# Ordering every engine queue of a chunked-attention and MLP kernel with a list scheduler inside the kernel, and loading v as fp32 with a cast on GpSimd

## The chip, the cores and the metric

The kernel runs on one core of a Trainium2 chip. The time is the device time of one execution in microseconds (us). "Before" has a median of 350.23 us in three executions (348.98 to 351.46). Ratios below are the mean time of one kernel's fast runs over the mean time of the other's fast runs of the same rounds, with a 95% interval, so they are not quite the ratios of the medians that are quoted beside them.

Engines are named as in the profile: PE is the matrix engine (TensorE), PEld its weight loads, DVE is VectorE, ACT is ScalarE, POOL is GpSimd, SP is SyncE, which here only starts transfers. "Granted clock" is the share of full speed that the throttle of PE allowed. The trace records it from some time after the start only (from 12.4 us in "before"), and the views count the time before that as full clock, although the matmuls there take the durations of half clock. A matmul's end is modelled by the profiler, so distances below are taken from start to start.

The profiled execution of "before" took 353.15 us and is marked slow, about 3 us above the median. So about 3 us of any difference between the two traces may be that.

## The reference

```python
# q, k, v: [4, 8, 768, 64] fp32;  w_in: [512, 2048];  w_out: [2048, 512]
k_min, k_max = min and max of k over each chunk of 32 keys         # 24 chunks
ub  = sum_d max(q * k_min, q * k_max)          # bound of each query for each chunk
ub  = where(chunk of the query >= chunk, ub, -1e9)
sel = the 6 chunks with the largest ub
p   = softmax(q k^T / 8, over selected chunks and keys <= query)
x   = (p v), as [3072, 512]
h   = x @ w_in;   g = h * clip(h + 3, 0, 6) / 6
return g @ w_out
```

Heads are worked on in pairs: there are 16 pairs, four for each batch. For a pair there are these steps, named by a letter in the code: K and Q (transpose the loaded tile, make the chunk minimum and maximum, and the positive and negative parts of q), U (bound matmuls), V (transpose the bounds back, then the top six on DVE), L (transpose the selection and copy it beside q), S (scores, three tiles a head, then exp on ACT and the causal mask on GpSimd) and P (probabilities times v). The MLP of a batch can start when all four pairs of that batch are done. It fills PE while the attention of the next batch goes on.

## The kernel before

Only PE has an order of its own. It is written by hand: lists of attention steps, between which a quota of MLP items is drawn. The order of the other engines is left to the framework. MLP items come only from the second batch on.

```python
ctx.enter_context(tc.manual_schedule(engines={mybir.EngineType.PE}))
...
ORDER = [("S", 0, 0, 0), ("L", 1), ("S", 0, 0, 1), ("P", -1, 1), ("M",), ("U", 2), ...]
FIRST = [("K", 0), ("Q", 0), ("U", 0), ("K", 1), ("V", 0), ("Q", 1), ("L", 0)]
START = [("S", 0, 0, 0), ("U", 1), ("S", 0, 0, 1), ("K", 2), ("V", 1), ...]
...
def run_slot(steps, quota):
    total = sum(c for c, _ in steps)
    done = acc = 0.0
    for c, f in steps:
        f()
        done += c
        while mlp and acc < quota * done / total:   # MLP work, paced by the quota
            cm, fm = mlp.pop(0)
            fm()
            acc += cm
```

The three places where the change also alters the data path:

```python
def load_v(i):                      # v: two transfers a pair, cast to bf16 on the way, GpSimd's queue
    ...
    for e in range(2):
        nc.gpsimd.dma_start(VB[:, e, :, 0:D], v[b, 2 * hp + e].rearrange("(blk p) d -> p blk d", p=P))

    # end of step_Q: the q rows of the score operand, copied on DVE
    for e in range(2):
        nc.vector.tensor_copy(s["RHS"][e][0:D, :], QTS[e * D:(e + 1) * D, 0:S])

def step_L(i):                      # three transposes of 128 columns, four copies
    s = st[i]
    SLT = ps_sm.tile([P, QH], BF16, name="SLT", tag="ps")
    for t in range(NT):
        n = min(P, QH - t * P)
        nc.tensor.transpose(SLT[:, t * P:t * P + n],
                            s["SEL"][0:n, t].rearrange("p h e c -> p (h e c)"), IDENTB[0:n, 0:n])
    with tc.high_priority(offset=HI):
        for h in range(2):
            for e in range(2):
                r = (2 * h + e) * CH
                nc.vector.tensor_copy(s["RHS"][e][D:D + NCH, P + h * QH:P + (h + 1) * QH], SLT[r:r + NCH, :])
```

The softmax here doesn't subtract the row's maximum and nothing guards it: scores larger than these inputs give would overflow.

Of the kernel before, what the change touches and what calls it, by code (L numbers as in the profile page):

```python
# [15 lines left out]
P = 128  # L16
CH = 32
TOPK = 6
BIG = 50.0
E_VAL = 8.0 * BIG  # L20


@with_exitstack
def kernel(
# [21 lines left out]
    NSB = NBLK - 1  # L46
    assert D == 64 and S == 768 and H % 2 == 0 and TOPK * CH >= P
    scale = 1.0 / np.sqrt(D)

    const = ctx.enter_context(tc.tile_pool(name="const", bufs=1))  # L50
    ps_big = ctx.enter_context(tc.tile_pool(name="ps_big", bufs=3, space=bass.MemoryType.PSUM))
    ps_sm = ctx.enter_context(tc.tile_pool(name="ps_sm", bufs=2, space=bass.MemoryType.PSUM))
    src = ctx.enter_context(tc.tile_pool(name="src", bufs=4))
    xpool = ctx.enter_context(tc.tile_pool(name="xpool", bufs=2))
    work = ctx.enter_context(tc.tile_pool(name="work", bufs=2))
    ptpool = ctx.enter_context(tc.tile_pool(name="ptp", bufs=9))
    small = ctx.enter_context(tc.tile_pool(name="small", bufs=4))
    gt_pool = ctx.enter_context(tc.tile_pool(name="gtp", bufs=2))
    u_pool = ctx.enter_context(tc.tile_pool(name="up", bufs=3))
    o_pool = ctx.enter_context(tc.tile_pool(name="op", bufs=3))  # L60

    ctx.enter_context(tc.manual_schedule(engines={mybir.EngineType.PE}))
# [3 lines left out]
    loads = {}  # L66

    def load_qk(i):
        b, hp = pairs[i]
        KS = src.tile([P, NBLK, 2, D], FP32, name="KS", tag="ks")  # L70
        QS = src.tile([P, NBLK, 2, D], FP32, name="QS", tag="qs")
        for t, x in ((KS, k), (QS, q)):
            for e in range(2):
                nc.sync.dma_start(t[:, :, e, :], x[b, 2 * hp + e].rearrange("(blk p) d -> p blk d", p=P))
        loads[i] = [KS, QS, None]

    def load_v(i):
        b, hp = pairs[i]
        VB = VB_tiles[i % NVB]
        for e in range(2):  # L80
            nc.gpsimd.dma_start(VB[:, e, :, 0:D], v[b, 2 * hp + e].rearrange("(blk p) d -> p blk d", p=P))
        loads[i][2] = VB

    IDENT32 = const.tile([P, P], FP32, name="IDENT32")
    load_qk(0)
    make_identity(nc, IDENT32[:])
    QH = NSB * P // 2
    NT = -(-QH // P)
    EMASK = const.tile([P, 2, 2, NCH], FP32, name="EMASK")
    nc.vector.memset(EMASK[:], 0.0)  # L90
    nc.vector.memset(EMASK[0:D, :, 0, :], 1.0)
    nc.vector.memset(EMASK[D:P, :, 1, :], 1.0)
    IDENTB = const.tile([P, P], BF16, name="IDENTB")
    nc.vector.tensor_copy(IDENTB[:], IDENT32[:])
    NEGBIG = const.tile([P, 1], FP32, name="NEGBIG")
    nc.vector.memset(NEGBIG[:], -BIG)
    THREE = const.tile([P, 1], FP32, name="THREE")
    nc.vector.memset(THREE[:], 3.0)
    load_qk(1)

    E128 = const.tile([P, S], BF16, name="E128")
    nc.gpsimd.memset(E128[:], E_VAL)
    nc.gpsimd.affine_select(out=E128[:], in_=E128[:], pattern=[[1, S]],
                            compare_op=A.is_ge, fill=0.0, base=32 * 64,
                            channel_multiplier=-32)
    nc.gpsimd.affine_select(out=E128[:], in_=E128[:], pattern=[[-1, S]],  # L106
                            compare_op=A.is_ge, fill=0.0, base=-32 * 64 + 31,
                            channel_multiplier=32)
    BIAS = const.tile([P, NT, 2, 2, NCH], FP32, name="BIAS")
    nc.gpsimd.memset(BIAS[:], 0.0)  # L110
    for t in range(NT):
        nc.gpsimd.affine_select(out=BIAS[:, t], in_=BIAS[:, t], pattern=[[QH, 2], [0, 2], [-CH, NCH]],
                                compare_op=A.is_ge, fill=-1e9, base=P + t * P, channel_multiplier=1)
    NVB = 6
    VB_tiles = []
    for i in range(NVB):
        VT = const.tile([P, 2, NBLK, D + 1], BF16, name=f"VB{i}")
        nc.vector.memset(VT[:, :, :, D:D + 1], 1.0)
        VB_tiles.append(VT)
    load_v(0)  # L120
    NOP = 8
    LHS_tiles, RHS_tiles, SEL_tiles, KC_tiles, UBS_tiles = [], [], [], [], []
    for i in range(4):
        Kt = const.tile([P, 2, 2, CH], FP32, name=f"KC{i}")
        nc.vector.memset(Kt[:], 0.0)
        KC_tiles.append(Kt)
    for i in range(2):
        Ut = const.tile([P, NT * P], FP32, name=f"UBT{i}")
        nc.vector.memset(Ut[:, QH:NT * P], 0.0)
        UBS_tiles.append(Ut)  # L130
    for i in range(NOP):
        Lt = const.tile([P, S], BF16, name=f"LHS{i}")
        eng = nc.vector if i < 2 else nc.gpsimd
        eng.tensor_copy(Lt[D:D + NCH, :], E128[D:D + NCH, :])
        LHS_tiles.append(Lt)
        Rt = const.tile([P, S], BF16, name=f"RHS{i}")
        nc.vector.memset(Rt[D:D + NCH, 0:P], 1.0)
        RHS_tiles.append(Rt)
    for i in range(2):
        St = const.tile([P, NT, 2, 2, CH], BF16, name=f"SEL{i}")  # L140
        nc.vector.memset(St[:], 0.0)
        SEL_tiles.append(St)

    WIN = const.tile([P, KT_HID, DFF], BF16, name="WIN")
    WOUT = const.tile([P, FT, DMODEL], BF16, name="WOUT")
    wo = moe_w_out.rearrange("(f p) m -> p f m", p=P)

    weight_loads = []
    for kt in range(KT_HID):
        weight_loads.append(lambda kt=kt: nc.gpsimd.dma_start(WIN[:, kt, :], moe_w_in[kt * P:(kt + 1) * P, :]))  # L150
    for f0 in range(0, FT, 4):
        weight_loads.append(lambda f0=f0: nc.gpsimd.dma_start(WOUT[:, f0:f0 + 4, :], wo[:, f0:f0 + 4, :]))

    def pair_transpose(SRC, name):
        T = ps_big.tile([P, 1024], FP32, name=name, tag="big")
        for j in range(NBLK):
            nc.tensor.transpose(T[:, j * P:(j + 1) * P], SRC[:, j].rearrange("p e d -> p (e d)"), IDENT32[:])  # L157
        return T

    HI = 100  # L160
    st = [dict() for _ in range(NP)]
    X_tiles = [None] * B

    def step_K(i):
        s = st[i]
        KT = pair_transpose(loads[i][0], "KT")
        if i == 0:
            KTS = KT
        else:
            KTS = work.tile([P, S], FP32, name="KTS", tag="kts")  # L170
            nc.scalar.copy(KTS[:], KT[:, 0:S])  # L171
        KM = small.tile([P, 2, 1, NCH], FP32, name="KM", tag="km")
        view = KTS[:, 0:S].rearrange("p (c w) -> p c w", w=CH)
        nc.vector.tensor_reduce(out=KM[:, 0, 0, :], in_=view, axis=AX.X, op=A.max)  # L174
        nc.vector.tensor_reduce(out=KM[:, 1, 0, :], in_=view, axis=AX.X, op=A.min, negate=True)  # L175
        KC = KC_tiles[i % 4]
        nc.vector.tensor_tensor(out=KC[:, :, :, 0:NCH], in0=KM[:].to_broadcast([P, 2, 2, NCH]), in1=EMASK[:], op=A.mult)
        s["KC"] = KC
        s["LHS"] = [LHS_tiles[(2 * i + e) % NOP] for e in range(2)]
        if i == 0:  # L180
            s["KT"] = KT
        else:
            for e in range(2):
                nc.gpsimd.tensor_copy(s["LHS"][e][0:D, :], KTS[e * D:(e + 1) * D, :])

    def step_Q(i):
        s = st[i]
        QT = pair_transpose(loads[i][1], "QT")
        QP = work.tile([P, NSB * P], FP32, name="QP", tag="qp")
        QN = work.tile([P, NSB * P], FP32, name="QN", tag="qn")  # L190
        if i == 0:
            QTS = QT
            nc.scalar.activation(QP[:], QT[:, P:S], ACT.Relu)
            nc.scalar.activation(QN[:], QT[:, P:S], ACT.Relu, scale=-1.0)
            for e in range(2):
                nc.scalar.copy(s["LHS"][e][0:D, :], s["KT"][e * D:(e + 1) * D, 0:S])
        else:
            QTS = work.tile([P, S], FP32, name="QTS", tag="qts")
            nc.scalar.copy(QTS[:], QT[:, 0:S])  # L199
            nc.vector.tensor_scalar(out=QP[:], in0=QTS[:, P:S], scalar1=0.0, scalar2=None, op0=A.max)  # L200
            nc.vector.tensor_scalar(out=QN[:], in0=QTS[:, P:S], scalar1=-1.0, scalar2=0.0,
                                    op0=A.mult, op1=A.max)
        s["QP"], s["QN"] = QP, QN
        s["RHS"] = [RHS_tiles[(2 * i + e) % NOP] for e in range(2)]
        for e in range(2):
            nc.vector.tensor_copy(s["RHS"][e][0:D, :], QTS[e * D:(e + 1) * D, 0:S])

    def step_U(i):
        s = st[i]
        KC = s["KC"]  # L210
        UBP = ps_sm.tile([P, QH], FP32, name="UBP", tag="ps")
        for n, X in enumerate((s["QP"], s["QN"])):
            for h in range(2):
                nc.tensor.matmul(UBP[h * 2 * CH:(h + 1) * 2 * CH, :], lhsT=KC[:, n].rearrange("p e c -> p (e c)"),  # L214
                                 rhs=X[:, h * QH:(h + 1) * QH], start=(n == 0), stop=(n == 1))
# [234 lines left out]
```

## Time and profile before

Lines of the page of "before": the busy time of each engine with its share of the span, and then the span in 40 slices of 8.8 us each. A digit is the busy share in tenths; for PEclk it is the granted clock in tenths.

```profile
span 351.4 us, 6082 instructions
PE 306.9 (87%) x2336; PEld 182.1 (52%) x2336; DVE 210.8 (60%) x572; ACT 192.5 (55%) x235; POOL 106.8 (30%) x185
PE   3576689859899998998899999998899999899995
POOL 9958554550422314241324231220202111000000
PEclk9858688887999999999999999999999999999999
DMA  9999999990324615262512200000001000100102
```

PE is the bound: it is busy 87% of the span, and no other engine is above 60%. But its row has two parts. In the first nine slices, to about 78 us, PE is at 3 to 9 tenths and its clock at 5 to 9, and DMA is full. After that PE is at 8 or 9. The border is the first hidden matmul of the MLP, HP. The view by timeline shows it; the columns are start in us, duration in us, engine, line, operation, output and inputs, count, and in brackets the idle time before and what ended it. The second line belongs to the last P step of the attention.

```profile
78.44 1.97 PE L329 MATMUL HP<-XT,WIN 128*128 128x384 bf16 x5
...
300.07 0.68 PE L293 MATMUL PVP<-VB_138,PT 128*128 128x65 bf16 x16 [0.55 <-POOL PT L276]
```

This gives three stages: the start (to the first HP), the middle (to the end of the last P step) and the tail (MLP alone). For each stage "work" is an estimate: PE's instruction order in the trace, times what each group takes from start to start where PE runs without waits at full clock. The values are 1.30 us for 8 hidden matmuls, 0.865 for 4 output matmuls, 0.66 for the six transposes of K or Q, 1.22 for a pair's bound matmuls, 0.38 for a score tile, 0.665 for a head's P step, and 0.34 for the three selection transposes. "Loss" is the length of the stage less the work. It holds waits, gaps, and slow execution at half clock. Both are estimates: a recount of the matmuls with these values agrees to within 1.4 us a stage. The values leave out the 48 transposes of the bounds (109 ns each from start to start) and the 96 of x (56 ns), 10.6 us of work. With them the losses of start and middle are 41.9 and 24.3 us in "before".

| before | length | work | loss |
|---|---|---|---|
| start, to the first HP at 78.4 us | 78.4 | 32.9 | 45.5 |
| middle, to 300.7 us | 222.3 | 191.8 | 30.5 |
| tail | 50.7 | 46.4 | 4.3 |

So by this count 76 of the 80 us that PE loses are lost before the tail, and more than half of them in the first quarter of the span. What PE waits for is in the view of waits of PE: the engine and line that waits, what it waits for, then us in total, number of waits, longest wait.

```profile
PE SLT L245 <- DVE SEL_190 L235: 7.8, 2, 4.6
PE HP L329 <- ACT PT L273: 6.9, 9, 1.1
PE KT L157 <- DMA KS<-in_k_dram: 4.8, 1, 4.8
PE PVP L293 <- POOL PT L276: 4.7, 4, 1.4
```

In the start the selection on DVE is late (7.8 us in two waits, and 2.5 in a third, for SEL_192, that is not shown), the first K tile comes at 4.8 us, and the masks on GpSimd are late. In the middle the hidden matmuls wait for the exp that frees their PSUM buffer (6.9 us in nine waits). The view by windows tells how full the engines are. Its columns are the window, its length, then busy us (and instructions) of PE, PEld, DVE, ACT and POOL, then the granted clock, the DMA share and GB/s.

```profile
0.00:30.00 30.00, 15.96 (x75) 10.09 (x75) 20.01 (x76) 12.51 (x16) 25.19 (x41) 0.83 1.41 190
30.00:70.00 40.00, 32.50 (x292) 21.33 (x293) 31.65 (x112) 22.61 (x29) 22.25 (x37) 0.79 1.33 195
```

From 30 to 70 us no engine is full: DVE is busy 31.65 of 40 us, ACT and GpSimd 22. Such a picture suggests that the order is at fault, since each engine waits for another in turn. The transfers are full here (DMA at 9 in the row above), but PE waits for one only at the very start (4.8 us, and 0.3 for the first Q). The clock here is 0.79. Finally, two groups of DVE instructions and two DMA queues that matter later.

### The profile page before, as it was taken

What the parts mean: (1) busy time and instruction counts of PE and PEld (TensorE: products, weight loads), DVE (VectorE), ACT (ScalarE), POOL (GpSimd) and SP (SyncE); (2) the same over time, 40 slices, a digit from 0 to 9 for tenths busy, and PEclk for the clock granted to TensorE, in tenths of its full rate; (3) what the DMA queues carried; (4) which work ended last, traced back from release to release, by engine and by line L of the source; (5) the groups of instructions that cost most, each with busy time, mean ns of one, the idle gap of its engine ahead of it and who ended that gap; (6) DMA issues with size and microseconds to landing.
All of it is one profiled execution on the core that took longest, in us unless ns stands there. A gap on an engine that the chain in (4) does not pass through costs nothing.

```text
span 351.4 us, 6082 instructions
## 1 busy us (share of the span) xinstructions
PE 306.9 (87%) x2336; PEld 182.1 (52%) x2336; DVE 210.8 (60%) x572; ACT 192.5 (55%) x235; POOL 106.8 (30%) x185
## 2 busy tenths in 40 slices
PE   3576689859899998998899999998899999899995
PEld 2344455534555556554656465554655565464552
DVE  7749768882784569474866379464963462272340
ACT  2434576643565677544765477545755684262541
POOL 9958554550422314241324231220202111000000
PEclk9858688887999999999999999999999999999999
DMA  9999999990324615262512200000001000100102
GB/s 174 197 190 196 198 188 189 213 151 0 57 46 79 127 13 102 41 132 41 101 12 43 42 32 2 32 30 32 0 2 57 34 2 30 45 18 30 62 8 82
DMA packets 81437, 26.61 MB, mean 76 GB/s; under 512 B 75776, under 2 KB 77824, under 8 KB 81408
## 3 DMA queue, kind: packets, MB, share of 16 engines
q1 hardware_dynamic: 53632, 18.88, 24.2%
q0 software_dynamic: 27776, 7.34, 20.5%
q8 instruction: 18, 0.29, 0.4%
q14 instruction: 11, 0.09, 0.1%
HBM read 27.26 MB, written 6.29 MB: 95 GB/s over the span
## 4 chain that ended last, share of the span: by engine, by line
PE 74%; DVE 11%; ACT 8%; issue 3%; POOL 2%; DMA 1%; POOLq 0%; SPq 0%; DVEq 0%; ACTq 0%
PE HP L329 23%; PE OP L343 23%; PE UBP L214 7%; PE SPS L267 7%; PE PVP L293 6%; ACT PT L273 4%; ACT U L332 3%; PE KT L157 3%; DVE KM L174 1%; DVE KM L175 1%; PE UBQ L223 1%; PE QT L157 1%; PE SLT L245 1%; PE XTP L319 1%; DMA KS<-in_k_dram 1%
## 5 line engine op out<-in xcount | busy, mean ns | idle before, releaser
L273 ACT ACTIVATE PT<-SPS,NEGBIG 128x896 bf16<-128x896 f32 x96 | 93.7, 1009 | 32.6 <-PE SPS L267 32.4
L329 PE MATMUL HP<-XT,WIN 128*128 128x384 bf16 x512 | 94.4, 332 | 8.7 <-ACT PT L273 6.9
L343 PE MATMUL OP<-WOUT,GT 128*128 128x512 bf16 x384 | 92.4, 379 | 1.1 <-ACT UBT_156 L217 1.0
L333 DVE SCALAR_TENSOR_TENSOR GT<-U,HP 128x768 bf16<-128x768 bf16 x64 | 61.0, 953 | 50.5 <-ACT U L332 49.6
L276 POOL TENSOR_SCALAR_AFFINE_SELECT PT<-PT 128x256 bf16<-128x256 bf16 x96 | 40.9, 428 | 165.7 <-ACT PT L273 165.1
L332 ACT ACTIVATE U<-HP,THREE 128x768 bf16<-128x768 f32 x64 | 57.6, 900 | 48.9 <-PE HP L329 48.9
L329 PEld LDWEIGHTS <-WIN 128*128 128x128 bf16 x512 | 49.5, 99 | 42.8 <-issue 15.0
L343 PEld LDWEIGHTS <-GT 128*128 128x128 bf16 x384 | 35.7, 97 | 38.7 <-issue 4.6
L293 PEld LDWEIGHTS <-PT 128*128 128x128 bf16 x672 | 26.8, 101 | 11.3 <-POOL PT L276 5.8
L347 ACT ACTIVATE OT<-OP 128x512 f32<-128x512 f32 x24 | 14.3, 595 | 28.2 <-PE OP L343 27.6
L225 DVE TENSOR_TENSOR UBS<-UBQ,BIAS 128x288 f32<-128x288 f32 x16 | 7.3, 457 | 34.4 <-PE UBQ L223 34.4
L157 PE MATMUL KT<-IDENT_90,KS 128*128 128x128 f32 x96 | 15.9, 310 | 4.8 <-DMA KS<-in_k_dram 4.8
L297 DVE TENSOR_TENSOR Xb<-PVP,RINV 128x384 bf16<-128x384 f32 x32 | 17.8, 555 | 0.7
L199 ACT COPY QTS<-QT 128x768 f32<-128x768 f32 x15 | 12.0, 801 | 8.9 <-PE QT L157 8.8
L174 DVE TENSOR_REDUCE KM<-KTS 128x24 f32<-128x768 f32 x15 | 14.2, 950 | 4.4 <-ACT KTS L171 4.3
L157 PEld LDWEIGHTS KT<-IDENT_90,KS 128*128 128x128 f32 x96 | 12.8, 160 | 7.2 <-POOL E_117 L106 4.7
L296 DVE RECIPROCAL RINV<-PVP 128x6 f32<-128x6 f32 x32 | 6.1, 192 | 15.5 <-PE PVP L293 15.2
L171 ACT COPY KTS<-KT 128x768 f32<-128x768 f32 x15 | 12.0, 799 | 4.6 <-PE KT L157 4.6
L175 DVE TENSOR_REDUCE KM<-KTS 128x24 f32<-128x768 f32 x15 | 14.2, 945 | 0.1
L157 PE MATMUL QT<-IDENT_90,QS 128*128 128x128 f32 x96 | 13.9, 283 | 0.3 <-DMA QS<-in_q_dram 0.3
L322 DVE COPY XT<-XTP 128x768 bf16<-128x768 bf16 x16 | 8.6, 552 | 7.1 <-PE XTP L319 7.0
L157 PEld LDWEIGHTS QT<-IDENT_90,QS 128*128 128x128 f32 x96 | 11.5, 146 | 1.9 <-issue 0.7
(176 smaller groups left out, 357.0 us busy)
## 6 DMA issues: line engine op xcount, KB each, us to landing
KS<-in_k_dram SPq DMA_DIRECT2D x32, 192.0 KB, 4.8
QS<-in_q_dram SPq DMA_DIRECT2D x32, 192.0 KB, 4.5
out_dram<-OT SPq DMA_DIRECT2D x24, 256.0 KB, 2.0
WIN<-in_moe_w_in_dram POOLq DMA_DIRECT2D x4, 512.0 KB, 10.6
WOUT<-in_moe_w_out_dram POOLq DMA_DIRECT2D x4, 512.0 KB, 14.1
VB_132<-in_v_dram POOLq DMA_DIRECT2D x6, 96.0 KB, 5.5
VB_134<-in_v_dram POOLq DMA_DIRECT2D x6, 96.0 KB, 5.0
VB_136<-in_v_dram POOLq DMA_DIRECT2D x6, 96.0 KB, 5.3
```

The lines of the kernel that those rows point to most:

```text
L157: nc.tensor.transpose(T[:, j * P:(j + 1) * P], SRC[:, j].rearrange("p e d -> p (e d)"), IDENT32[:])
L174: nc.vector.tensor_reduce(out=KM[:, 0, 0, :], in_=view, axis=AX.X, op=A.max)
L214: nc.tensor.matmul(UBP[h * 2 * CH:(h + 1) * 2 * CH, :], lhsT=KC[:, n].rearrange("p e c -> p (e c)"), rhs=X[:, h * QH:(h + 1) * QH], start= ...
L267: nc.tensor.matmul(SPS[:, base + c:base + c + n], lhsT=LHS[0:K, j * P:(j + 1) * P], rhs=RHS[0:K, j * P + c:j * P + c + n], start=True, sto ...
L273: nc.scalar.activation(PT[:, 0:base], SPS[:, 0:base], ACT.Exp, bias=NEGBIG[:], scale=scale)
L276: nc.gpsimd.affine_select(out=dv, in_=dv, pattern=[[0, 2], [1, P]], compare_op=A.is_ge, fill=0.0, base=0, channel_multiplier=-1)
L293: nc.tensor.matmul(PVP[:, qb, :], lhsT=PT[:, loc:loc + P], rhs=VB[:, e, j, :], start=(j == 0), stop=(j == qb))
L297: nc.vector.tensor_tensor(out=Xb[:, :, h * D:(h + 1) * D], in0=PVP[:, :, 0:D], in1=RINV[:].to_broadcast([P, NBLK, D]), op=A.mult)
L329: nc.tensor.matmul(HP[:, f, 0:GRP], lhsT=WIN[:, kt, (f0 + f) * P:(f0 + f + 1) * P], rhs=XT[:, kt, :], start=(kt == 0), stop=(kt == KT_HID ...
L332: nc.scalar.activation(U[:], HP[:, :, 0:GRP], ACT.Relu, bias=THREE[:], scale=1.0)
L333: nc.vector.scalar_tensor_tensor(out=GT[:, f0:f0 + 2, :], in0=U[:], scalar=6.0, in1=HP[:, :, 0:GRP], op0=A.min, op1=A.mult)
L343: nc.tensor.matmul(OP[:, :], lhsT=GT[:, f, t * P:(t + 1) * P], rhs=WOUT[:, f, :], start=(f == 0), stop=(f == FT - 1))
```

## The change

The intent is to let one model decide the order of all queues. Every operation gets an engine, a duration (most taken from measurements), a key that says how urgent it is, what it depends on, and which buffers of which ring it takes and uses. The scheduler then goes through simulated time. On each engine it takes the operation that can start first; on PE, of all those that can start within 0.1 us, it takes the one with the lowest key. The resulting order is emitted and binds PE, DVE, ACT, GpSimd and SP. MLP items have keys that pace them through the attention of the next batch, so they fill whatever PE would otherwise wait. This is the core of the diff, much cut:

```diff
-    ctx.enter_context(tc.manual_schedule(engines={mybir.EngineType.PE}))
+    E = mybir.EngineType
+    ctx.enter_context(tc.manual_schedule(engines={E.PE, E.DVE, E.Activation, E.Pool, E.SP}))
+    rings = dict(big=3, sm=2, ks=3, qs=3, vb=3, vs=3, kts=2, ..., pt=9, x=4, xt=2, gt=2, u=3, ot=2)
+    plan = Plan(rings, dict(PE=2.0, DVE=3.2, ACT=2.2, POOL=5.0, LD=0.8, ST=0.0))
 ...
+    def run(self, slack):
+        ...
+                for op in lst:
+                    r = self.ready(op)          # dependences, latencies, ring buffers
+                    if r is None:
+                        continue
+                    at = max(r, self.free[eng])
+                    s = slack.get(eng, 0.0)
+                    if mine is None or (at + s < mine[0]) or (at < mine[0] + s and op.key < mine[1].key):
+                        mine = (at, op)
 ...
-            nc.gpsimd.dma_start(VB[:, e, :, 0:D], v[b, 2 * hp + e].rearrange("(blk p) d -> p blk d", p=P))
+        def castv():
+            nc.gpsimd.tensor_copy(fx(s["vb"])[:, :, :, 0:D].rearrange("p e k d -> p k e d"), s["vs"].obj[:])
+        lv = add("LD", 2.07, i - 3.2 , lambda: ld(s["vs"], v, "VS"), take=[s["vs"]], chain="ldv")
+        s["o_v"] = add("POOL", 0.85, i + 0.3, castv, deps=[lv], take=[s["vb"]], use=[s["vs"]], chain="castv")
 ...
-            nc.vector.tensor_copy(s["RHS"][e][0:D, :], QTS[e * D:(e + 1) * D, 0:S])
+    RHS_NAME, RHS_DUR, RHS_ENG = "POOL", 0.84, nc.gpsimd.tensor_copy
 ...
-        SLT = ps_sm.tile([P, QH], BF16, name="SLT", tag="ps")       # 3 transposes, 4 copies of 24x320
+            T = new(sl, [2 * CH, NSB * P], BF16, "SLT")             # 6 transposes, 2 copies of 24x640
+            for h in range(2):
+                for t in range(NT):
+                    n = min(P, QH - t * P)
+                    c = h * QH + t * P
+                    nc.tensor.transpose(T[:, c:c + n], fx(s["sel"])[0:n, t, h].rearrange("p e c -> p (e c)"),
+                                        IDENTB[0:n, 0:n])
```

So there are four parts: the plan with all queues bound to it; v as fp32 through SP's queue with a cast on GpSimd; the q copies moved from DVE to GpSimd; and six smaller selection transposes with two larger copies. The first part is the idea. The other three are called "the data paths" below.

## The prediction

> What bounds the kernel now: TensorE (chain of waits: PE 74% of the span; page: PE busy 87%). PE's ordered work times start-to-start pitches at full clock from the timeline (8 hidden matmuls 1.30 us, 4 output matmuls 0.865, six K or Q transposes 0.66, a pair's bound matmuls 1.2, score tile 0.38, a head's PV 0.66) gives 272 us. The span is 351.4, so 79 us are lost:
> - Before the first MLP matmul at 78.4 us PE does 33 us of that: 45 lost. There is only attention then, 10.5 us a pair, against 8 us of ACT work a pair (six exps of 1.01, two copies of 0.8, one of 0.43). The windows give a granted clock of 0.67 to 0.86 from 10 to 90 us; the Trainium skill (TensorE: Matmul & The Clock Gate, "The HAM clock gate") says a little-used PE drops to half clock, and here the bound matmuls do take 2.3 us against 1.2. PE also waits for the selection on DVE (10.3 us), GpSimd's masks (4.7) and the first load (4.8).
> - From 78 to 302 us PE does 193 us in 224: 31 lost in short waits (hidden matmuls behind the exp that frees their PSUM, 6.9) and small gaps.
> - From 302 us a dense MLP: 45 us of work in 49, tail included. PE's order there is unchanged.
>
> What the change does. PE work stays 272 us; selection transposes become 6 small ones for 3. It moves:
> - v: 24,576 packets of 128 B with cast, 31.8 ns each, become 256 B ones at about 22 ns (as K and Q): 15 us less DMA in all, 1 us a pair; DMA is over 90% busy until 78 us. GpSimd gains a cast of about 0.85 us a pair and loses two DMA issues of 0.84.
> - Two q copies a pair (0.55 to 0.95) go from DVE to GpSimd (0.82 each); four selection copies of 0.32 become two of about 0.5. DVE falls from about 8.5 to 6.7 us a pair, GpSimd comes to 6.7: below ACT's 8, but nearly full in the start.
> - Order: each queue takes the lowest-key work able to start, so PE fills waits with MLP, and the first selection no longer stands behind second-pair work on DVE. The first hidden matmul comes after 37 us of PE work, not 33. Load rings are 3 deep, on one queue; weights follow on GpSimd's.
>
> Estimate. Start: GpSimd about 50 us after its constants, DMA 50 to 60 us for what is needed, ACT 45 us from its first copy, PE at a mixed clock (the plan's durations are full-clock): first MLP matmul at 65 us (58 to 74), with 235 us of PE work left. Before did the rest at 87.5%; I expect 94 to 95%: 249 us. Predicted 314 us, range 300 to 330. Faster by over 2%: 0.94; within 2%: 0.05; slower: 0.01.
>
> What would show it. (1) First hidden matmul at 58 to 74 us. (2) Clock below 0.9 before it, 1.0 after. (3) From there to the last attention matmul, PE's loss falls from 31 us to about 12, hidden-after-exp waits mostly gone. (4) Last 47 us unchanged. (5) GpSimd busy up by some 13 us, DVE down by some 24; DMA packet time down 10%.
>
> What would make it wrong. GpSimd in order behind a v cast whose load is late, stalling masks: masks show as PE's releaser and the start is no shorter (330 or more). A real order differing from planned durations (half clock), so that in-order queues block one another. Or better: a plan that keeps the clock up in the start gives 298.

## More of the kernel before

For the groups the columns are count, busy us and mean ns of one, then idle before; for the queues they are packets, MB, and the share of 16 engines' span.

```profile
L201 DVE TENSOR_SCALAR QN<-QTS 128x640 f32<-128x640 f32 x15 | 7.6, 509 | 0.0
L200 DVE TENSOR_SCALAR QP<-QTS 128x640 f32<-128x640 f32 x15 | 7.5, 501 | 4.0 <-ACT QTS L199 4.0
...
q1 hardware_dynamic: 53632, 18.88, 24.2%
q0 software_dynamic: 27776, 7.34, 20.5%
```

## The result, and the profile after

"After" takes 327.42 us (median of 4, 327.3 to 327.95). "Before" took 350.85 us in the same rounds (348.98 to 352.46). The ratio is 0.9337, 95% interval 0.9287 to 0.9387: faster. The page of "after", the same lines as above, with slices of 8.2 us:

```profile
span 326.2 us, 6154 instructions
PE 302.9 (93%) x2384; PEld 180.8 (55%) x2384; DVE 197.3 (60%) x505; ACT 192.8 (59%) x235; POOL 122.4 (38%) x201
PE   3569898998999999998999999999999899999995
POOL 8477998950364204361234252652112120000000
PEclk9989999999999999999999999999999999999999
DMA  9999999989363124370143200000001001000101
```

PE is busy for nearly the same time (302.9 us against 306.9), in a shorter span. Its row reaches 9 in the fourth slice and stays at 8 or 9 until the last slice. The clock row is at 9 but for one slice (the first two slices have no clock record and run at half clock, as said above). GpSimd is at 7 to 9 from the third to the eighth slice, where it was mostly at 4 or 5. The border lines of the stages, in the timeline:

```profile
69.41 4.06 PE L532 MATMUL HP<-XT,WIN 128*128 128x384 bf16 x24
...
274.59 0.82 PE L470 MATMUL PVP<-VB_117,PT 128*128 128x65 bf16 x21
```

| after | length (change) | work (change) | loss (change) |
|---|---|---|---|
| start, to 69.4 us | 69.4 (-9.0) | 39.0 (+6.1) | 30.4 (-15.1) |
| middle, to 275.3 us | 205.9 (-16.4) | 192.2 (+0.4) | 13.7 (-16.8) |
| tail | 50.9 (+0.2) | 46.4 (0.0) | 4.5 (+0.2) |

The sum closes: 15.1 and 16.8 us less loss, 6.6 us more work (rounded over the stages) and 0.2 more in the tail give 25.1 us; the spans differ by 25.2. The start holds 6.1 us more work because the plan puts more attention ahead of the MLP and because the selection transposes cost more (below). The waits of PE, the longest of "after":

```profile
PE KT L275 <- DMA KS<-in_k_dram: 4.7, 1, 4.7
PE UBP L356 <- DVE KC_120 L300: 2.7, 1, 2.7
PE UBP L356 <- DVE KC_121 L300: 2.7, 1, 2.7
...
PE HP L532 <- DVE GT L542: 2.1, 2, 1.2
PE HP L532 <- ACT PT L441: 1.0, 2, 0.7
```

The selection is no longer among them (0.4 us is left), nor are the masks. The first two bound matmuls now wait for the chunk statistics on DVE, 5.4 us together, against 1.4 in "before". Hidden matmuls behind exps fell from 6.9 us in nine waits to 1.0 in two. The first load (4.7) is as it was. The windows of the start:

```profile
0.00:30.00 30.00, 18.55 (x87) 10.97 (x88) 20.11 (x68) 11.94 (x15) 20.68 (x35) 0.94 1.25 206
30.00:70.00 40.00, 36.10 (x387) 24.85 (x388) 35.14 (x108) 33.33 (x41) 36.86 (x59) 1.00 1.09 202
```

From 30 to 70 us four engines are now nearly full at once: PE 36.1 of 40 us, DVE 35.1, ACT 33.3, GpSimd 36.9. In the same window of "before" they were at 32.5, 31.7, 22.6 and 22.3. The same work flows through with fewer mutual waits, while the transfers are full in both (DMA at 9 to 79 us in "before", and at 8 or 9 to 82 us in "after"). The groups and queues that answer to those shown of "before":

```profile
L330 DVE TENSOR_SCALAR QN<-QTS 128x640 f32<-128x640 f32 x15 | 14.7, 981 | 0.0
L332 DVE TENSOR_SCALAR QP<-QTS 128x640 f32<-128x640 f32 x15 | 10.6, 704 | 2.4 <-ACT QTS L321 2.3
...
q1 hardware_dynamic: 78720, 25.17, 35.9%
q0 software_dynamic: 2688, 4.19, 7.5%
```

Two instructions that the change did not touch became slower: the negative and positive parts of q on DVE went from 509 and 501 ns to 981 and 704. That is 10.2 us of DVE time that the prediction did not have. The packets' time fell from 44.7% of 351.4 us to 43.4% of 326.2 us on 16 engines, which is 10% less.

### The profile page after: what moved, and what is told of

Its sections match the earlier page's. It is cut to its first block, busy times and chain, and to the rows that moved or that the text cites. A ratio compares the mean times of both kernels' runs of the same rounds, so it can differ in the third digit from the quotient of the medians.

```text
span 326.2 us, 6154 instructions
## 1 busy us (share of the span) xinstructions
PE 302.9 (93%) x2384; PEld 180.8 (55%) x2384; DVE 197.3 (60%) x505; ACT 192.8 (59%) x235; POOL 122.4 (38%) x201
## 4 chain that ended last, share of the span: by engine, by line
PE 75%; DVE 14%; ACT 6%; issue 1%; DMA 1%; POOL 1%; SPq 0%; ACTq 0%; DVEq 0%
PE OP L556 26%; PE HP L532 22%; PE SPS L435 7%; PE UBP L356 6%; PE PVP L470 5%; ACT PT L441 4%; DVE KM L294 3%; PE SLT L408 3%; PE KT L275 2%; PE QT L275 2%; DVE QP L332 1%; DVE QN L330 1%; PE XTP L512 1%; DMA KS<-in_k_dram 1%; ACT U L536 1%
## 5 line engine op out<-in xcount | busy, mean ns | idle before, releaser
L441 ACT ACTIVATE PT<-SPS,NEGBIG 128x896 bf16<-128x896 f32 x96 | 91.8, 1010 | 9.8 <-PE SPS L435 9.5
L532 PE MATMUL HP<-XT,WIN 128*128 128x384 bf16 x512 | 89.8, 326 | 3.3 <-DVE GT L542 2.1
L556 PE MATMUL OP<-WOUT,GT 128*128 128x512 bf16 x384 | 87.8, 379 | 0.0
L556 PEld LDWEIGHTS <-GT 128*128 128x128 bf16 x384 | 36.9, 98 | 40.6
L562 ACT ACTIVATE OT<-OP 128x512 f32<-128x512 f32 x24 | 14.3, 597 | 51.4 <-PE OP L556 42.9
L470 PEld LDWEIGHTS <-PT 128*128 128x128 bf16 x672 | 25.4, 97 | 4.0 <-POOL LHS_124 L307 0.5
L275 PE MATMUL KT<-IDENT_108,KS 128*128 128x128 f32 x96 | 14.9, 296 | 5.4 <-DMA KS<-in_k_dram 4.7
L275 PEld LDWEIGHTS KT<-IDENT_108,KS 128*128 128x128 f32 x96 | 11.7, 151 | 7.9 <-POOL BIAS L230 4.6
L249 POOL CAST VB_117<-VS 128x768 bf16<-128x768 f32 x6 | 5.2, 874 | 26.7 <-PE PVP L470 26.7
L275 PE MATMUL QT<-IDENT_108,QS 128*128 128x128 f32 x96 | 14.8, 294 | 0.3 <-DMA QS<-in_q_dram 0.3
L330 DVE TENSOR_SCALAR QN<-QTS 128x640 f32<-128x640 f32 x15 | 14.7, 981 | 0.0
```

The lines of the kernel that those rows point to most:

```text
L275: nc.tensor.transpose(T[:, j * P:(j + 1) * P], src.obj[:, j].rearrange("p e d -> p (e d)"), IDENT32[:])
L330: nc.vector.tensor_scalar(out=o[:], in0=i_, scalar1=-1.0, scalar2=0.0, op0=A.mult, op1=A.max)
L441: nc.scalar.activation(T[:, 0:base], sp.obj[:, 0:base], ACT.Exp, bias=NEGBIG[:], scale=scale)
L470: nc.tensor.matmul(T[:, qb, :], lhsT=t[:, c:c + P], rhs=fx(s["vb"])[:, e, j, :], start=(j == 0), stop=(j == qb))
L532: nc.tensor.matmul(T[:, f, 0:GRP], lhsT=WIN[:, kt, (f0 + f) * P:(f0 + f + 1) * P], rhs=xt.obj[:, kt, :], start=(kt == 0), stop=(kt == KT_H ...
L556: nc.tensor.matmul(T[:, :], lhsT=gt.obj[:, f, t * P:(t + 1) * P], rhs=WOUT[:, f, :], start=(f == 0), stop=(f == FT - 1))
```

## The experiments

Two questions are left by the comparison. First, which parts of the change bring the gain: the plan for PE, the plan for the other queues, or the data paths? Second, is the slow start of "before" caused by the low clock, or is the low clock only a mark of a PE that waits? Twelve runs were made, each timed in three or five rounds. All gave correct results. The stages of all of them, in one table (us, from each run's profiled execution; the first two rows are the kernels themselves):

| run | what it is | median | span | start (loss) | middle (loss) |
|---|---|---|---|---|---|
| before | | 350.85 | 351.4 | 78.4 (45.5) | 222.3 (30.5) |
| after | | 327.42 | 326.2 | 69.4 (30.4) | 205.9 (13.7) |
| a1_slt3 | after, three selection transposes | 325.05 | 323.4 | 70.1 (33.5) | 202.3 (14.2) |
| a2_qdve | after, q copies on DVE | 331.75 | 330.0 | 72.2 (33.5) | 206.8 (14.3) |
| a3_vcast | after, v cast in the transfer | 331.83 | 330.0 | 86.3 (37.2) | 192.4 (10.3) |
| a4_peonly | after, only PE bound to the plan | 336.75 | 335.2 | 78.0 (38.9) | 206.2 (14.1) |
| e3_plan_only | plan, all three old data paths | 330.36 | 328.8 | 76.0 (37.7) | 201.6 (15.1) |
| b2_v | before, new v path | 360.39 | 357.7 | 85.2 (52.3) | 221.8 (30.0) |
| e4_data_only | before, all three new data paths | 367.16 | 365.6 | 90.1 (54.7) | 224.8 (29.0) |
| b1_warm | before, idle PE work in the start | 347.90 | 348.6 | 74.7 | 223.2 |
| c2_warm | a1 with idle PE work in the start | 323.46 | 321.0 | 67.7 | 202.3 |
| c3_deps | c2 with another order for pair 0 | 324.66 | 322.1 | 68.8 | 202.3 |
| d_after2 | after again | 328.12 | 326.7 | 69.9 | 205.8 |
| d_c2b | c2 again, same chip as d_after2 | 324.23 | 322.7 | 69.8 | 201.9 |

The tail was 50.7 to 51.3 us in all of them. Where a run adds idle work, or where only the length matters, no loss is given. Each row is one execution, and the start scatters: c2_warm and d_c2b are the same kernel, and their first HP comes at 67.7 and 69.8 us.

### a1_slt3: three selection transposes again

```diff
-            T = new(sl, [2 * CH, NSB * P], BF16, "SLT")
-            ... six transposes of 64 columns ...
+            T = new(sl, [P, QH], BF16, "SLT")
+            ... three transposes of 128 columns, as before ...
-                nc.vector.tensor_copy(fx(s["rhs"])[e][D:D + NCH, P:S], sl.obj[e * CH:e * CH + NCH, :])
+                for h in range(2):
+                    r = (2 * h + e) * CH
+                    nc.vector.tensor_copy(fx(s["rhs"])[e][D:D + NCH, P + h * QH:P + (h + 1) * QH], sl.obj[r:r + NCH, :])
```

> The changed kernel with the old form of the selection transposes: three 128-column ones a pair instead of six 64-column ones, and four selection copies instead of two (the scheduler plans with 0.66 us for two of them). Theory: the six small transposes cost PE 0.74 us start to start where three cost 0.34, 16 times, 6.3 us given back by the change; with PE the bound after the start, this run gains 5 to 7 us: 321 to 323 us. Rival: PE has slack that hides it, or the 0.33 us of DVE work a pair that comes back matters as much: within 2 us of 327.4.

Measured: 325.05 us (324.95 to 325.31), ratio 0.9239 (0.9204 to 0.9275) to "before", which took 352.44 us in these rounds. The timeline shows what the transposes cost. First "after", six of them and the next work; then a1_slt3, three of them and the same next work:

```profile
48.42 0.81 PE L408 MATMUL SLT<-IDENTB,SEL_143 128*64 128x128 bf16 x6
49.17 0.55 PE L372 MATMUL UBQ<-IDENT_108,UBT_140 128*128 128x128 f32 x3
```

```profile
31.33 0.41 PE L406 MATMUL SLT<-IDENTB,SEL 128*128 128x128 bf16 x3
31.66 0.55 PE L372 MATMUL UBQ<-IDENT,UBT 128*128 128x128 f32 x3
```

From start to start that is 0.75 us against 0.33: on average a transpose of 64 columns takes 125 ns and one of 128 columns 111 ns. Halving the columns saves nothing and the count doubles. Over 16 pairs this is 16 x (0.75 - 0.34) = 6.6 us of PE work, with the 0.34 that most of the groups of three show. The measured gain, 2.4 us, lies between the theory's 5 to 7 and the rival's 2. It is smaller than the work saved, as the middle shows (205.9 to 202.3 us, 3.6 less) and the start does not (69.4 and 70.1 us). So PE work is worth its time in the middle, where PE is the bound; in the start, by these two traces, it is worth nothing that can be seen.

### a2_qdve: q copies back on DVE

```diff
-    RHS_NAME, RHS_DUR, RHS_ENG = "POOL", 0.84, nc.gpsimd.tensor_copy
+    RHS_NAME, RHS_DUR, RHS_ENG = "DVE", 0.58, nc.vector.tensor_copy
```

> The changed kernel with the q copies back on DVE (planned at 0.58 us each). Theory: the move to GpSimd gained little, because the copies on GpSimd slow DVE's two-valued relu pair (0.70 and 0.98 us a pair, against 0.50 and 0.51 before) and fill GpSimd to over 90% from 30 to 70 us: this run is within 2 us of 327.4, GpSimd busy drops to about 95 us, the relu pair comes back to near 0.5 us each. Rival: the relief of DVE is a main part of the gain: 331 us or more.

Measured: 331.75 us (330.62 to 332.04), ratio 0.9422 (0.9374 to 0.9469). The theory fell and the rival held: the move is worth about 4 us (medians of 331.75 and 327.42, of different rounds), although it slows other work on DVE. The groups of a2_qdve:

```profile
L330 DVE TENSOR_SCALAR QN<-QTS 128x640 f32<-128x640 f32 x15 | 8.7, 582 | 0.0
L332 DVE TENSOR_SCALAR QP<-QTS 128x640 f32<-128x640 f32 x15 | 7.5, 503 | 11.6 <-ACT QTS L321 11.5
```

With the q copies on DVE, QN and QP take 582 and 503 ns; with the same copies on GpSimd they take 981 and 704. So the slowdown in "after" comes with GpSimd's copies running beside them. The single instructions in the trace of "after" say the same: the two QN that overlap no instruction of GpSimd take 476 and 477 ns, and eleven of the other thirteen take 1106 ns or more. The Trainium skill (GPSIMD Engine Reference, section 1, the row on SBUF interfaces) says that GpSimd shares its SBUF interfaces with VectorE, with contention when a DVE instruction runs in a 2-port mode or has two SBUF inputs. QN and QP have one input each, and the trace does not show their mode, so the slowdown fits this row without proving which condition held. The start still shows the gain: DVE is freed of 30 copies, and the start is 2.8 us shorter for it (72.2 against 69.4).

### a3_vcast: v cast in the transfer again

```diff
         def castv():
-            nc.gpsimd.tensor_copy(fx(s["vb"])[:, :, :, 0:D].rearrange("p e k d -> p k e d"), s["vs"].obj[:])
+            for e in range(2):
+                nc.gpsimd.dma_start(fx(s["vb"])[:, e, :, 0:D], natural(v, b, 2 * hp + e))
-        lv = add("LD", 2.07, i - 3.2 , lambda: ld(s["vs"], v, "VS"), take=[s["vs"]], chain="ldv")
-        s["o_v"] = add("POOL", 0.85, i + 0.3, castv, deps=[lv], take=[s["vb"]], use=[s["vs"]], chain="castv")
+        iv = add("POOL", 1.70, i - 1.0, castv, take=[s["vb"]], chain="castv")
+        s["o_v"] = add("LD", 3.05, i - 3.2, None, deps=[iv], use=[s["vb"]], chain="ldv")
```

(and six v buffers, not three)

> The changed kernel with v loaded as before, cast in the transfer and issued by GpSimd (six v tiles, planned as 1.7 us of GpSimd and 3.05 us of transfer). Theory: transfers stay saturated in the start (over 90% until about 73 us), and v costs about 1 us more a pair there, so the first hidden matmul comes 2 to 6 us later: 329 to 333 us. Rival: the start is bound by PE, ACT and GpSimd, not by transfers: within 1.5 us of 327.4.

Measured: 331.83 us (331.38 to 331.86), ratio 0.9428 (0.9391 to 0.9465). It is 4.4 us slower than "after". The time is in the range that the theory gave, but by luck: the first HP came 16.9 us later and not 2 to 6. The run is not a pure undo. The plan, told of longer loads, put 10.1 us more PE work ahead of the MLP (49.1 us against 39.0), so the first HP comes at 86.3 us, and the middle is 13.5 us shorter in return. In a kernel with such a plan, to change one operation is to change the whole order.

### a4_peonly: the plan binds PE alone

```diff
-    ctx.enter_context(tc.manual_schedule(engines={E.PE, E.DVE, E.Activation, E.Pool, E.SP}))
+    ctx.enter_context(tc.manual_schedule(engines={E.PE}))
```

> The changed kernel with only PE's queue in the planned order; DVE, ACT, GpSimd and the load queue are ordered by the framework's own scheduler, as in the kernel before. Theory: what the plan gains it gains through the order of PE (and the order in which the steps are written), so this run keeps most of it: 327 to 332 us. Rival: the planned order of the other queues is what gains: 338 us or more.

Measured: 336.75 us (336.53 to 337.23), ratio 0.9573 (0.9535 to 0.961), between the two expectations. The table tells the two stages apart. In the middle the loss is 14.1 us, as in "after" (13.7): there PE's order alone brings the gain. In the start the loss is 38.9 us against 30.4: about 8.5 of the 15.1 us saved there need the order of the other queues. The framework's order is still made from code that the plan emits in its own sequence, so this run shows what the binding adds, and not all that the plan does for those queues.

### b1_warm: idle work to keep the clock up, on "before"

```diff
         SLT = ps_sm.tile([P, QH], BF16, name="SLT", tag="ps")
+        for _ in range(40 if i < 3 else 0):
+            nc.tensor.transpose(SLT[:, 0:P], IDENTB[:], IDENTB[:])
 ...
             for j in range(qb + 1):
+                if qb == 2 and j == 0 and e == 1 and i < 6:
+                    for _ in range(16):
+                        nc.tensor.matmul(PVP[:, 3, :], lhsT=IDENTB[:], rhs=IDENTB[:, 0:D + 1], start=True, stop=True)
```

> The kernel before, with PE kept busy where it waits in the start: 40 idle transposes of the identity ahead of each of the first three selection transposes, 16 idle matmuls inside the PV step of each second head of pairs 0 to 5 (their results are overwritten; the output stays right). Theory: half clock is a cause of the long start, not only its mirror: the clock stays at 1.0 for most of the start, the first hidden matmul comes at 68 to 73 us and not 78, and the time is 341 to 346 us. Rival: the start is bound by DVE, GpSimd and ACT, PE's clock only follows: 349 us or more, first hidden matmul at 77 us or later.

Measured: 347.9 us (345.58 to 350.3), ratio 0.9969 (0.9898 to 1.004), "before" 349.36 (one of seven slow): the same. The time and the first HP (74.7 us) lie between the two expectations, so neither held as it was written. Two rows of its page, PE and granted clock, and one of its waits of PE:

```profile
PE   3888887968899998997899998997999999899995
PEclk9989997878999999999999999999999999999999
...
PE QT L157 <- DMA QS<-in_q_dram: 2.5, 2, 2.2
```

The clock is up in the first six slices (9 9 8 9 9 9, where "before" has 9 8 5 8 6 8), and the time stays as it was. By the clock records, half clock before the first HP fell from 28.5 us to 11.5 us (without the time before the first record). So this much half clock accounts for at most about 1% of the time; what the rest costs is not shown.

The timelines show where the higher clock went. It did move PE forward: the first P step of the third pair starts at 52.5 us, against 59.0 in the trace of "before", about 3 us of which may be the slower state of that execution. Then PE waited 2.2 us for a load of q, which "before" did not, and the clock fell to half again from 56 us (7 and 8 in slices seven to ten); at the first HP 3.8 us of the lead were left. The idle work also has a price: the 16 matmuls take 0.5 us each time. So the run shows that half clock is not the main reason of the long start. It does not show that half clock costs nothing.

### b2_v and e4_data_only: the data paths without the plan

```diff
+        VS = src.tile([P, NBLK, 2, D], FP32, name="VS", tag="vs")
         for e in range(2):
-            nc.gpsimd.dma_start(VB[:, e, :, 0:D], v[b, 2 * hp + e].rearrange("(blk p) d -> p blk d", p=P))
+            nc.sync.dma_start(VS[:, :, e, :], v[b, 2 * hp + e].rearrange("(blk p) d -> p blk d", p=P))
+        nc.gpsimd.tensor_copy(VB[:, :, :, 0:D].rearrange("p e k d -> p k e d"), VS[:])
```

This is b2_v. The kernel e4_data_only has in addition the q copies of the pairs after the first on GpSimd, and six transposes with two copies, all on "before".

> The kernel before with the v change alone: v loaded as fp32 on the load queue, cast by GpSimd; the framework orders DVE, ACT, GpSimd and loads as it did. Theory: transfers end earlier but are not what the start waits for there, so 347 to 351 us. Rival: the v change is a main part of the gain by itself: 344 us or less.

> The kernel before, its own PE order and the framework's order elsewhere, with all three new data paths: v as fp32 and a GpSimd cast, q copies on GpSimd, six selection transposes and two copies. v alone made it 3.2% slower (360.4 us), because masks queued behind casts that wait for their load. Theory: GpSimd gets still fuller in the start and PE gains the 6.3 us of small transposes, so it is slower than before by 4 to 6%: 363 to 370 us. Rival: moving the q copies relieves DVE and brings it back to before or better: 352 us or less.

Measured: b2_v 360.39 us (358.72 to 361.61), ratio 1.0323 (1.0259 to 1.0387), so slower than "before"; both the theory and its rival missed this. After it, e4_data_only was expected to be slower and was: 367.16 us (365.36 to 368.55), ratio 1.0507 (1.0429 to 1.0585). The waits of GpSimd and PE in b2_v and then in e4_data_only:

```profile
POOL VB L83 <- DMA VS<-in_v_dram: 24.4, 6, 10.6
...
PE PVP L295 <- POOL PT L278: 9.4, 5, 5.5
```

```profile
POOL VB L83 <- DMA VS<-in_v_dram: 17.2, 3, 10.9
...
PE PVP L295 <- POOL PT L278: 15.7, 5, 7.6
```

GpSimd's cast waits for its load, up to 10.6 us, and the causal masks stand behind the cast in the same queue. So PE waits for masks 9.4 us (b2_v) and 15.7 us (e4_data_only), against 4.7 in "before". That is 4.7 of the 6.3 us, and 11.0 of the 14.2, by which these traces are longer than that of "before". The Trainium skill (TensorE: Matmul & The Clock Gate, the paragraph on engine queue depths) calls the queue of each of GpSimd's cores strict FIFO; these waits agree. In "after" the cast is ordered late, with key i + 0.3, when its load has long landed. There the cast waits for a free buffer instead, as the waits of GpSimd show:

```profile
POOL VB_117 L249 <- PE PVP L470: 26.7, 3, 13.5
```

That wait is off the critical path: P steps behind masks are not in the list of PE's longest waits.

### e3_plan_only: the plan with the old data paths

This is "after" with the edits of a1_slt3, a2_qdve and a3_vcast together.

> The planned order with the data paths of the kernel before: v cast in the transfer by GpSimd's queue, q copies on DVE, three selection transposes and four copies. Theory: the parts add up; single undos cost 4.4 us (v), 4.3 us (q) and -2.4 us (selection), so about 334 us (331 to 337), still 15 us or so under the kernel before: most of the gain is the order. Rival: the order needs the new data paths to work: 340 us or more.

Measured: 330.36 us (329.38 to 331.99), ratio 0.9464 (0.9406 to 0.9521). With d_after2 and e4_data_only, which ran on the same chip, this makes a table of two by two (medians, for "before" of its eight fast executions, since three of the eleven were slow; change to "before" in brackets). The time is a little below the 331 to 337 us that were expected, so the single undos do not add up:

| | framework's order | plan |
|---|---|---|
| old data paths | 348.82 | 330.36 (-18.5) |
| new data paths | 367.16 (+18.3) | 328.12 (-20.7) |

The verdict that came with the runs is "unclear" for e3_plan_only and e4_data_only; their intervals lie wholly beyond 2% all the same, and so does the difference between any two of the four medians but that of the plan's column, 330.36 and 328.12.

The plan brings 18.5 of the 20.7 us by itself. The data paths cost 18.3 us without it and bring 2.2 with it. They cannot be valued one by one outside the order in which they stand. "Plan" here means the whole of it: the order, which queues are bound, and its own buffer counts (for the loads of k and q three, where "before" had four). No run separates the buffer counts from the order. By stages: the plan takes the middle's loss from 30.5 to 15.1 with the old data paths and to 13.7 with the new, while e4_data_only stays at 29.0. In the start the loss is 45.5, 54.7 (data paths alone), 37.7 (plan alone) and 30.4 (both).

### c2_warm, c3_deps, and the pair d_after2 and d_c2b

The kernel c2_warm is a1_slt3 with idle fp32 transposes of a constant ahead of the first three steps that come after long waits of PE. The kernel c3_deps is c2_warm in which two copies of pair 0 must follow the chunk statistics and the negative part of q.

```diff
+    def fill(T, n):
+        for _ in range(n):
+            nc.tensor.transpose(T[:, 0:P], IDENT32[:], IDENT32[:])
 ...
+        fill(T, extra)                          # 13 ahead of the K step of pair 0
 ...
+            fill(T, {0: 22, 1: 28}.get(i, 0))   # ahead of the bound matmuls of pairs 0 and 1
```

```diff
-            ... deps=[up] + s["o_lhs"][:1],
+            ... deps=[up] + s["o_lhs"][:1] + ([s["o_kc"]] if direct else []),
 ...
-            ... deps=[up] + s["o_rhs"][:1], take=...
+            ... deps=[up] + s["o_rhs"][:1] + ([s["o_qn"]] if direct else []), take=...
```

> The run with three selection transposes (325.05 us), plus idle fp32 transposes on PE where it waits at the start: 13 before the first K transposes, 22 and 28 before the first two bound matmuls. Theory: the first steps then run at full clock and the two half-clock stretches after 20 us vanish: 320 to 323 us. Rival: the start hangs on DVE, ACT and GpSimd: 324.5 us or more.

> The run before in this list, plus two order constraints for pair 0 in the plan: ACT's copies of k after its relu pair, DVE's copies of q after the relu pair. In the changed kernel the second chunk reduce on DVE waits 1.7 us for ACT's copies from the same PSUM tile, and the second relu waits 1.9 us for DVE's copy, so the first bound matmul starts at 10.7 us against 9.2 in the kernel before. Theory: it starts at about 9 us again and the time falls by 1 to 2 us more: 319 to 322 us. Rival: the start is bound by work, not by this chain: no change.

Measured: c2_warm 323.46 us (322.73 to 325.01), ratio 0.9283 (0.9222 to 0.9345); c3_deps 324.66 us (323.89 to 325.96), ratio 0.9307 (0.9253 to 0.9361). These do not differ beyond the intervals, nor does either from a1_slt3. The time of c2_warm lies between its two expectations. That of c3_deps is as its rival said, but the run does not settle the order of pair 0: the first bound matmul starts at 9.5 us, against 9.9 in c2_warm and 10.7 in a1_slt3, but the 28 idle transposes after it ran at half clock, for 5.3 us and not 3.2, and the second bound matmul came later than in c2_warm (22.6 us against 21.4).

The last two runs put "after" and c2_warm on one chip, five rounds each.

> The changed kernel itself, to stand on the same chip as the last run of this list: 326 to 329 us on both theories.

> Three selection transposes and idle fp32 transposes on PE in the start (as run before, 323.5 us), beside the changed kernel on the same chip. Theory: 1% better than the changed kernel, 323 to 325 us, of which the mid part gives 3.5 us (trace: 202.3 against 205.8 us from first hidden matmul to last PV) and the start the rest. Rival: the gain was chip to chip spread: within 1.5 us of the changed kernel.

Measured: d_after2 328.12 us (327.26 to 328.41), ratio 0.9389 (0.9347 to 0.9431); d_c2b 324.23 us (322.29 to 326.42), ratio 0.9283 (0.9232 to 0.9334). So this version is 1.2% faster than "after" (324.23 / 328.12) and beats both kernels. The borders of its stages, its clock row and one wait of PE tell where that comes from:

```profile
PEclk9999999999999999999999999999999999999999
PE QT L280 <- DMA QS<-in_q_dram: 2.9, 2, 2.5
...
69.78 4.06 PE L538 MATMUL HP<-XT,WIN 128*128 128x384 bf16 x24
...
271.05 0.82 PE L476 MATMUL PVP<-VB,PT 128*128 128x65 bf16 x21
```

The clock is full from the first record, at 6.1 us, to the end; in d_after2 it is half until 17.6 us and for 6.8 us more. Still the first HP comes at 69.78 us, where d_after2 has it at 69.88. As in b1_warm, PE was ahead (a score step at 61.4 us, against 63.5) and then waited for a load of q, 2.5 us at 68.4 us; c2_warm, the same kernel without that wait, has its first HP at 67.7 us. So these single traces put a full clock at about 2 us in the start where no load is late, and in d_c2b nothing was left of it. The whole gain of d_c2b in these two traces is in the middle (201.9 us against 205.8), where most of the three transposes are, and not partly in the start, as its expectation said. Idle work has no gain that is clear of the noise; what beats "after" is a1_slt3's edit.

## Why the prediction was right or wrong

The time: 314 us predicted, 327.42 measured, inside the range of 300 to 330, and faster by more than 2% as given with 0.94. The centre was 13 us too low. Point by point, with the numbers of the prediction's own list:

1. The first hidden matmul at 58 to 74 us, 65 expected: it came at 69.4. Right, 4.4 us late.
2. "Clock below 0.9 before it": wrong by the windows, which give 0.94 to 30 us and 1.00 from there to 70 us. Apart from the cold beginning the clock records of "after" hold one stretch at half clock, 3.4 us long. With the beginning, before the first record, counted at half clock the mean to the first HP is 0.84 (0.74 in "before"), so the number came out on that count, but not for the reason given, a clock that stays mixed. The prediction also listed the low clock among the reasons for the slow start. b1_warm and d_c2b leave it a small part: raising the clock left the time of the one within noise (0.9898 to 1.004) and the first HP of the other where it was. The gate itself behaves as the Trainium skill (TensorE: Matmul & The Clock Gate, "The HAM clock gate") says, either half or full clock, in stretches that are here multiples of 3.41 us; but the low clock was more a consequence of waits than their cause.
3. Loss in the middle from 31 to about 12 us: measured 30.5 to 13.7, and hidden matmuls behind exps fell from 6.9 to 1.0 us. Right. a4_peonly (14.1) and e3_plan_only (15.1) show that this gain comes from PE's order and needs neither the binding of the other queues nor the data paths.
4. The tail unchanged: 50.7 and 50.9 us. Right.
5. GpSimd up by 13 us: up by 15.6 (106.8 to 122.4). DMA packet time down by 10%: down by 10%. Both right. DVE down by 24 us: down by 13.5 (210.8 to 197.3). Wrong, by 10.5 us, because QN and QP slowed by 10.2 us beside a busy GpSimd, as a2_qdve shows.

The terms of the sum that were mis-sized: the prediction took 65 us for the start and then 249 us for the rest (235 us of work at 94 to 95%, so 14 us of loss), 314 in all. The span is 326.2 us, 12.2 more, and three terms make that up.

- The start took 69.4 us, 4.4 more.
- The work of the rest was 192.2 + 46.4 = 238.6 us, 3.6 more. The step that failed here is "PE work stays 272 us; selection transposes become 6 small ones for 3". Six transposes of 64 columns take 0.75 us and three of 128 columns 0.34, so the work is 277.6 us in all and not 272. The prediction counted "small" as "cheap". Of the 6.6 us that these transposes add, six of the 16 groups (2.5 us) lie in the start and ten (4.1 us) in the middle, where a1_slt3 got back 3.6 us by undoing it.
- The loss of the rest was 13.7 + 4.5 = 18.2 us, 4.2 more. Half of this was in the prediction's own sum: it expected 12 us of loss in the middle and left the tail's 4 (45 us of work in 49) as it was, which is 16 and not 14.

The listed risk came true in a way: "GpSimd in order behind a v cast whose load is late, stalling masks" is just what b2_v and e4_data_only do. The plan avoids it. The other risk, that real durations differ from planned ones so that bound queues block one another, did not show: binding all queues (after) beats binding PE alone (a4_peonly) by 9.3 us between the two medians.

The comparison also gives where the gain of the data paths went. The costs in the prediction were nearly all right (packets, busy times), but the sum of the three paths is only 2.2 us with the plan, because the six transposes give back 2.4 us (a1_slt3), and probably because the slowed QN and QP give back more; what these cost in time was not measured.

What stays open: the 30.4 us that are lost in the start of "after". From 30 to 70 us, PE, DVE, ACT and GpSimd are all busy 33 to 37 of 40 us, and the transfers are full to 82 us. Less PE work (a1_slt3, first HP at 70.1 us), a higher clock (c2_warm 67.7, d_c2b 69.8) and another order of pair 0 (c3_deps, 68.8) moved its end by about 2 us at most, which is the scatter of one kernel. To shorten it, one would probably have to take work from several engines at once; that was not tried, nor was it tested how much of the start the transfers hold, though PE's waits for q in b1_warm and d_c2b point there. Nor can the value of the v path alone under the plan be told, since a3_vcast also changed the order.

## What to carry to other kernels

When no engine is full and the critical one still waits, suspect the order: one model that orders all queues can be worth more than local changes. Here it was 18.5 us, against 2.2 for three data-path changes that by themselves cost 18.3. A queue that works in order, as GpSimd's did here, must not be given work whose input may be late in front of work that others wait for. Count matrix instructions and not their size when small transposes are split, and look at what a moved copy does to its neighbours, since an instruction that nobody touched may slow down to nearly twice its time.

## What the Trainium skill lacked or had wrong

- GPSIMD Engine Reference, section 1: it names the contention with VectorE on SBUF but gives no size there. Other pages of the skill say more of it, so what was lacking is only the figure for these instructions. Here DVE's 128x640 fp32 tensor_scalar went from 509 to 981 ns (QN) and from 501 to 704 ns (QP) with copies running on GpSimd, and was back at 582 and 503 ns when those copies went to DVE.
- TensorE: Matmul & The Clock Gate, "Back-to-back issue gap": it gives about 81 ns for a sustained pair of weight load and matmul at N=128. The selection transposes took 111 to 113 ns each (three of 128 stationary columns) and 125 ns (six of 64). The page does not say what a switch between such short groups costs. Why these are slower than the page's figure was not tested.
- TensorE: Matmul & The Clock Gate, "The HAM clock gate": it speaks of an idle and a busy window of about 3.4 us, but not of the busy share that decides. The traces do not give it either. In windows of 3.41 us laid along the clock records, counted while the clock was full, "before" and "after" went to half clock after a busy share of PE of 0.60 or less and kept full clock at 0.63 or more; but windows of 0.42 (a4_peonly), 0.50 (d_after2) and 0.51 (d_c2b) kept it too, and one of 0.61 (b2_v) lost it.
